# Two decode layers in one kernel: P times V of layer one in the wide form, its buffers in one arena slot, and the score mask as one matmul

## The chip, the cores and the metric

The kernel runs on one core of a Trainium2 chip. The metric is the device time of one execution in microseconds. It is compared as the median of several executions. The profile is one execution, seen by the hardware profiler; its span goes from the first to the last instruction of the program.

## What is computed

Two identical layers over a batch of four single tokens (`B = 4`, `Sq = 1`, `D = 512`), each an attention over a sliding window of a cached K and V and then a gated feed-forward block:

```python
W = min(4096, max(256, Sk // 4))          # 2048 of 8192 positions
rep = Hq // Hkv                           # 32 query heads, 8 kv heads: 4
q = (x @ wq) ...                          # 32 heads of 128
k = jnp.repeat(k_cache[:, :, Sk - W:, :], rep, axis=1)
v = jnp.repeat(v_cache[:, :, Sk - W:, :], rep, axis=1)
scores = einsum("bhqd,bhkd->bhqk", q, k) * (Dh ** -0.5)
p = softmax(scores, axis=-1)
o = einsum("bhqk,bhkd->bhqd", p, v) ... @ wo
...
x = x + A(layernorm(x));  x = x + B(layernorm(x))    # and both once more
# B: h = sigmoid(x @ w_gate) * (x @ w_up);  h @ w_down      (F = 1792)
```

The inputs are bfloat16. Both layers read the same cache and the same weights.

## The kernel before

**Data.** One head's K for all four tokens is two tiles of 1 MB (one a pair of tokens), the same for V. All of K (16 MB) is kept on the chip for both layers in its own 32 half tiles ("slots") of the `arena`. The other 18 slots make nine tiles, which `_SlotPool` gives out in turn to the query weights, V, the output projection `wo` (four tiles of two heads each, kept for both layers) and the feed-forward weights. Layer two runs the heads backwards and takes a few V tiles that layer one left in place; one V tile is put aside in PSUM during the feed-forward block ("stash": four transposes by DVE, line 568, and two half ones, line 585).

**The DMA queue.** All loads are issued by SP from line 398, in the order of one list (`loads`). `fill` takes loads from its head as long as a slot is free; a load whose slot is still read waits on SP for the last reader's semaphore, and everything behind it waits too. Around the end of layer one there are no free tiles, and some loads have a fixed place (`homes`): the two halves of the tiles named `Y`, `Z` (V of the last head), `GA` and `GB` (the two tiles of the first gate weights). The list of layer one goes: V of head 6, V of head 7 (two tiles each), gate weights (two tiles), up weights (four halves), down weights (four pieces), then the query weights of layer two.

**The order of the work.** The kernel emits operations in a program order; `_schedule` then simulates the engines with estimated durations and gives each engine its own order, which is fixed in the program. An operation with an earlier start goes first, one with an earlier place in the program wins a tie. Operations on one PSUM bank from different engines are ordered by `banks=`.

**Layer one** (`attn_first`). For each head h: DVE transposes K in place (`k_transpose`, line 830, four operations); the query is spread (line 818, ACT copies it, line 823); four mask matmuls (line 848) and sixteen score matmuls (line 859) of 32 columns with 512 moving columns fill one PSUM bank; DVE takes the maximum (lines 872 to 884), ACT the exponential (line 887); `turn_p` permutes P by a matmul (line 900), copies it (ACT, line 902) and transposes it (DVE, line 907). The sums go through four small GpSimd operations, three matmuls (line 926) and a reciprocal (line 933). The loop runs two heads ahead: `front(h + 2)`, then P times V of head h, then `turn` of head h + 2, then the output projection of head h.

P times V of layer one is **narrow** (`pv_unit`, line 949): for each pair of tokens 32 matmuls with a 128 x 128 block of V as the stationary operand and 8 columns of P moving; then a product with the reciprocals (DVE, line 957), four matmuls (line 967), a masked product (DVE, line 972) and 16 matmuls of the output projection (`wo_unit`, line 1137), which all heads add up in bank `WB`.

**Layer two** uses the **wide** form for seven of its eight heads (`pv_wide`, line 1033): 16 matmuls with 32 columns of P stationary and 512 columns of V moving, for both pairs at once; then a transpose of the bank (DVE, line 1041), a reduction (1046), a copy across partitions (1048), two GpSimd operations (`ad` 1050, `av` 1053), two small matmuls (`tr`, 1067), an ACT copy (1073) and four wide matmuls of the output projection (`wo_wide`, 1086). When the last of these is done, `wo_copy` (ACT, 1113) and `wo_back` (four fp32 matmuls, 1123) bring the result back to bank `WB`; the last heads use `wo_compact` (line 1102). The sums of the wide form (`sums`) need one GpSimd operation, one fp32 matmul (1008), a reciprocal (1010) and one more GpSimd operation (`rm`, 1013). Its buffers (`wide_buffers`) are doubled and lie in a tile of query weights that is no longer needed.

Of the kernel before, what the change touches and what calls it, by code (L numbers as in the profile page):

```python
# [278 lines left out]
def build(nc, A_x, A_k, A_v, A_wq, A_wo, B_wg, B_wu, B_wd, out, cfg=None):  # L279
# [16 lines left out]
    NJ = W // 128  # L296
# [25 lines left out]
    with es:  # L322
# [19 lines left out]
        msk_s = sb("msk_s", [128, 32], BF16)  # L342
        msk_m = sb("msk_m", [128, 2], BF16)
        psm = sb("psm", [128, 2], F32)
        rinv = sb("rinv", [128, 2 * NR], F32)
        onb = sb("onb", [128, 2 * NR], BF16)
        onp = sb("onp", [128, 2 * REP * NR], BF16)
# [73 lines left out]
        GB = ("wg", 1, 0)  # L421
# [122 lines left out]
        def load_glu(k):  # L544
            for nm, src in (("wg", wg_d), ("wu", wu_d)):
                if k == 0 and nm == "wu":
                    for c in range(NC):
                        load_half((nm, c, k), src[:, c, :], "bw_3k", F, ((Y, 0), (Y, 1), (Z, 0), (GA, 0))[c])
                    continue
                for cc in range(NC // 2):  # L550
                    load((nm, cc, k), 2, "bw_3k", (2 * F, src[:, 2 * cc:2 * cc + 2, :], False))
            on_free[GA] = lambda s: hfree.add(s + 1)
            on_free[GB] = lambda s: hfree.add(s + 1)
            for (a, b) in bounds_of(k):
                if k == 0:
                    load_half(("wd", a, k), wd_d[:, a:b, :].rearrange("p k n -> p (k n)"), "bw_4k", (b - a) * D,
                              ((GA, 1), (GB, 0), (GB, 1), (Y, 0))[a // 4])
                else:
                    load(("wd", a, k), 1, "bw_8k", ((b - a) * D, wd_d[:, a:b, :], False))
# [55 lines left out]
        P.op("vector", "zero_o", 1100.0, lambda v: v.memset(ps[:, OBS[0]:WB + 1, :], 0.0), w=[("o0",)], banks=OBS + (WB,))  # L615
# [3 lines left out]
        for jh in range(2):  # L619
            for bp in range(2):  # L620
                for i in range(2):
# [10 lines left out]
             lambda g: g.affine_select(msk_s[:, :].rearrange("p (i y) -> p i y", i=2),  # L632
                                       ones_f[:, :].rearrange("p (i y) -> p i y", i=2),
                                       [[1, 2], [0, NR]], ALU.is_equal, 0.0, base=-1, channel_multiplier=1),
# [202 lines left out]
        def softmax_unit(tag, hk, wait=False, q=True, between=None):  # L837
# [7 lines left out]
            def e_m(pe):  # L845
                last = None
                for gi in range(4):
                    last = pe.matmul(ps[32 * gi:32 * gi + 32, bank, :], msk_s[:, :],  # L848
                                     msk_m[:, :].unsqueeze(1).broadcast_to([128, 256, 2]), start=True, stop=False)
                return last  # L850

            def e_s(pe):
                last = None if wait else e_m(pe)
                for cp in range(4):
                    for gi in range(4):
                        jh, bp = gi // 2, gi % 2
                        kt = kpair(hk, bp).rearrange("p (j c k t) -> p c t j k", c=2, k=32, t=2)
                        q0 = ((k2 * 4 + cp) * 2 + bp) * 32
                        last = pe.matmul(ps[32 * gi:32 * gi + 32, bank, :], qbd[:, q0:q0 + 32],  # L859
                                         kt[:, cp // 2, cp % 2, jh * NJ:(jh + 1) * NJ, :], start=False, stop=(cp == 3))  # L860
                return last
# [36 lines left out]
        def turn_p(L, tag, k2, pb, wide=False):  # L898
# [10 lines left out]
            if L == 0:  # L909
                sums_old(tag, k2)  # L910

        def sums_old(tag, k2):
# [18 lines left out]
            rv = rinv[:, k2 * NR:(k2 + 1) * NR]  # L931
# [4 lines left out]
        def pv_unit(tag, h, k2, tiles, between=None):  # L936
            ob = OBS[k2]
            ev = ebuf[:, k2 * 256:(k2 + 1) * 256].bitcast(BF16).rearrange("p (m x t) -> p t m x", x=32, t=2)
            for n, (bp, name) in enumerate(tiles):
# [4 lines left out]
                def e_pv(pe, s=s, bp=bp):  # L944
                    last = None
                    src = tile_ap(s)
                    for j in range(2 * NJ):
# [7 lines left out]
            ov = onb[:, k2 * NR:(k2 + 1) * NR]  # L955
# [4 lines left out]
                     rinv[:, k2 * NR:(k2 + 1) * NR].rearrange("p (b r) -> p b r", r=REP), ALU.mult),  # L960
                 r=[("pso", k2, bp) for bp in range(2)] + [("rinv", k2)], w=[("on", k2)], banks=(ob,))
            op = onp[:, k2 * REP * NR:(k2 + 1) * REP * NR]
# [18 lines left out]
        def wide_buffers(s, op):  # L981
            f = tile_ap(s).bitcast(F32)
            n = 0
            for name, size in (("tv", 512), ("o32", 32), ("osh", 32), ("rm", 64), ("rv", 8), ("pr", 8)):
                for k2 in range(2):
# [4 lines left out]
            for k2 in range(2):  # L990
                rest["A", k2] = f[:, n:n + 128].bitcast(BF16)
                n += 128
            rest["op"] = op
            rest["mb"] = f[:, n:n + 64]
            P.op("gpsimd", "mb", 200.0,
                 lambda g: g.tensor_copy(rest["mb"].rearrange("p (b x) -> p b x", b=2),
                                         maskb.unsqueeze(2).broadcast_to([128, 2, 32])),
                 r=[("maskb",)], w=[("mb",)], after=(op,))

        def sums(tag, k2):  # L1000
            pr, rv, rm = (rest[n, k2] for n in ("pr", "rv", "rm"))
            P.op("gpsimd", "pr" + tag, 200.0,
                 lambda g: g.tensor_scalar(pr, sel_r[:, :], psm[:, k2:k2 + 1], None, ALU.mult),
                 r=[("psm", k2), ("sel_r",)], w=[("pr", k2)], after=(rest["op"],))
            sbank, c0 = (CB, 256) if tag in ("2.0", "2.%d" % (NW - 1)) else (WB, k2 * 8)
            out_ = ps[0:64, sbank, c0:c0 + 8]
            P.op("tensor", "sb" + tag, tm["pe_f32"],
                 lambda pe: pe.matmul(out_, rest["mb"], pr, start=True, stop=True),
                 r=[("pr", k2), ("mb",)], w=[("psb", k2)], banks=(sbank,))
            P.op("vector", "ri" + tag, c_dve(8) + 60.0, lambda v: v.reciprocal(rv[0:64, :], out_),  # L1010
                 r=[("psb", k2)], w=[("rinv", k2)], banks=(sbank,))
# [4 lines left out]
                 r=[("rinv", k2), ("maske",)], w=[("rm", k2)])  # L1016

        def pv_wide(tag, h, k2, tiles):
# [19 lines left out]
            for bp, name in tiles:  # L1038
                done(name)
            tv, o32, osh, rm, av = (rest[n, k2] for n in ("tv", "o32", "osh", "rm", "A"))  # L1040
            P.op("vector", "tv" + tag, c_dve(512), lambda v: v.transpose(tv, ps[:, ob, :]),  # L1041
                 r=[("pso", k2, 0), ("pso", k2, 1)], w=[("tv", k2)], banks=(ob,), after=(rest["op"],))

            def e_rd(v):
                dg = rest["dg", k2].rearrange("p (m y) -> p m y", m=4)[:, :, 0:128].rearrange("p m (q z) -> p q z m", z=32)[:, :, 0:8, :]
                return v.tensor_reduce(o32.rearrange("p (q x) -> p q x", x=8), dg, AXX, ALU.add)
            P.op("vector", "rd" + tag, c_dve(128), e_rd, r=[("tv", k2)], w=[("o32", k2)])
            P.op("vector", "sh" + tag, tm["dve_small"], lambda v: v.tensor_copy(osh[0:64, :], o32[64:128, :]),
                 r=[("o32", k2)], w=[("osh", k2)])
            P.op("gpsimd", "ad" + tag, 250.0, lambda v: v.tensor_tensor(o32[0:64, :], o32[0:64, :], osh[0:64, :], ALU.add),  # L1050
                 r=[("o32", k2), ("osh", k2)], w=[("o32", k2)])
# [5 lines left out]
                 r=[("o32", k2), ("rm", k2)], w=[("av", k2)])  # L1057
            late["tr", tag] = lambda: o_back(tag, k2, av)

        def o_back(tag, k2, av):  # L1060
            q0 = 16 + k2 * 16
            tb = CB if tag in ("2.%d" % (NW - 1), "2.%d" % (NW - 2)) else WB
# [7 lines left out]
            P.op("tensor", "tr" + tag, 2 * tm["pe_pair"], e_tr, r=[("av", k2), ("selm",)], w=[("pst", k2)], banks=(tb,))  # L1070
# [39 lines left out]
        def wo_copy():  # L1110
            k2 = (NW - 3) % 2
# [4 lines left out]
        def wo_back():  # L1116
            k2 = (NW - 3) % 2
            wr = rest["tv", k2]

            def e_b(pe):  # L1120
                last = None
                for c in range(NC):
                    last = pe.matmul(ps[:, WB, c * NR:c * NR + NB], wr[:, c * 128:(c + 1) * 128],
                                     selw[:, :], start=(c == 0), stop=False, skip_group_check=True)
# [21 lines left out]
        def attn_first():  # L1146
            def front(h):
                k_transpose(h)
                softmax_unit("0.%d" % h, h)
                turn = lambda: turn_p(0, "0.%d" % h, h % 2, PBS[h % 2])  # L1150
                return turn
# [3 lines left out]
            for h in range(HKV):  # L1155
                tag = "0.%d" % h
                turn = front(h + 2) if h + 2 < HKV else None
                if h == HKV - 1:
                    stash(stashed)
                    need(Z)  # L1160
                    stash_half(0, "st3")
                op = pv_unit(tag, h, h % 2, v_tiles[(0, h)])
                if turn is not None:
                    turn()
                wo_unit(tag, h, op, h % 2, False, h == HKV - 1)
# [102 lines left out]
        def glu(k, b0, b1, last=False):  # L1268
# [31 lines left out]
            for n, nm in enumerate(("wg", "wu")):  # L1300
                for c in range(NC):
                    piece = k == 0 and n == 1
# [12 lines left out]
                    if k == 0 and n == 0 and c % 2 == 0:  # L1315
# [106 lines left out]

        fill()
# [79 lines left out]
```

## Time and profile before

| | |
|---|---|
| device time, median of 3 executions | 181.05 us (180.65 to 181.91) |
| span of the profiled execution | 178.8 us |
| difference of the two | 2.25 us |
| bytes read from HBM | 70.78 MB |
| mean rate over the span | 396 GB/s |
| output of the kernel issued | 177.1 us into the span |

The device times are those of three executions; the page does not say which of them, if any, was profiled. In the slices of the page a digit is the busy share in tenths. The engines are PE (TensorE; its weight loads are a row of their own, PEld), DVE (VectorE), ACT (ScalarE), POOL (GpSimd) and SP (SyncE, which issues nearly all DMAs). The span has four parts: the query projection of layer one up to some 15 us; attention of layer one to 107 us; the feed-forward block to 118 us; layer two from there, whose attention ends at about 165 us.

### The profile page before, as it was taken

To read this page: it belongs to the slowest core of one execution; us is meant where nothing else is said; L and a number is where in the kernel's file an instruction comes from. 1 tells how busy PE (TensorE), PEld (TensorE's weight loads), DVE (VectorE), ACT (ScalarE), POOL (GpSimd) and SP (SyncE) were. 2 spreads that over 40 slices of the span, in tenths; PEclk is the share of its full clock that TensorE was granted. 3 is DMA by queue.
4 is the path that set the end of the run, shared out by engine and by line. 5 is a ranking of instruction groups with operands and counts; after the bars stand their busy time and mean duration, and the time that the engine had idled before them with its cause. 6 is when DMAs were issued, how large, how long until landed. Compare 5 with 4: busy or idle time off the path is not lost.

```text
span 178.8 us, 3879 instructions
## 1 busy us (share of the span) xinstructions
PE 101.7 (57%) x1641; PEld 55.1 (31%) x1653; DVE 104.4 (58%) x256; ACT 32.7 (18%) x87; POOL 21.5 (12%) x87
## 2 busy tenths in 40 slices
PE   0635326481933626506436857455886999766743
PEld 0202101241521412403414743231322444435311
DVE  7308997838476384593564483324199999751431
ACT  2002031221030300301102001000143455430101
POOL 6100010101010100100101000000011543351000
PEclk9999999999999999999999999999999999975555
DMA  5999999999999999999999999999999999999980
GB/s 184 418 429 427 422 423 416 414 422 420 422 413 419 420 423 422 411 421 422 423 411 420 414 401 387 407 360 421 410 395 418 423 420 422 412 418 402 410 353 22
DMA packets 12802, 71.05 MB, mean 397 GB/s; under 512 B 1256, under 2 KB 1264, under 8 KB 6640
## 3 DMA queue, kind: packets, MB, share of 16 engines
q1 hardware_dynamic: 12776, 70.79, 96.9%
q8 instruction: 13, 0.21, 0.5%
q14 instruction: 5, 0.04, 0.1%
q10 hardware_dynamic: 8, 0.00, 0.0%
HBM read 70.78 MB, written 0.00 MB: 396 GB/s over the span
## 4 chain that ended last, share of the span: by engine, by line
DMA 35%; DVE 33%; PE 19%; SPq 4%; issue 4%; ACT 2%; POOL 1%; DVEq 0%; ACTq 0%
DMA arena<-in_A_v_cache_dram 20%; DVE arena L830 11%; DMA arena<-in_B_w_down_dram 9%; PE ps L859 7%; DVE nmax L872 5%; DMA arena<-in_A_wq_dram 5%; SPq L398 4%; PE ps L949 3%; DMA arena<-in_B_w_up_dram 2%; PE ps L848 2%; DVE arena L1041 2%; DVE nmax L876 2%; DVE ebuf L907 2%; DVE mxt L880 2%; PE ps L1137 1%
## 5 line engine op out<-in xcount | busy, mean ns | idle before, releaser
L830 DVE STREAM_TRANSPOSE arena<-arena 128x1024 f32<-128x1024 f32 x32 | 37.0, 1202 | 0.0
L859 PE MATMUL ps<-arena,qbd 128*32 128x512 bf16 x256 | 25.8, 539 | 0.0
L949 PE MATMUL ps<-ebuf,arena 128*128 128x8 bf16 x576 | 17.8, 168 | 9.2 <-DMA arena<-in_A_v_cache_dram 6.1
L872 DVE TENSOR_REDUCE nmax<-ps 128x1 f32<-128x512 f32 x16 | 10.8, 676 | 19.9 <-PE ps L859 19.8
L848 PE MATMUL ps<-msk_m,msk_s 128*32 128x512 bf16 x64 | 8.6, 526 | 23.0 <-DVE arena L830 21.8
L949 PEld LDWEIGHTS ps<-ebuf,arena 128*128 128x128 bf16 x576 | 16.8, 104 | 11.3 <-DMA arena<-in_A_v_cache_dram 7.3
L887 ACT ACTIVATE prow<-ps,nmax 128x512 bf16<-128x512 f32 x16 | 11.0, 687 | 35.1 <-DVE nmax L884 29.5
L823 ACT CAST qbd<-ps 128x256 bf16<-128x256 f32 x16 | 5.9, 370 | 45.4 <-PE ps L859 35.2
L916 POOL CAST s<-psm 128x1 bf16<-128x1 f32 x9 | 1.7, 188 | 84.1 <-ACT prow L887 84.1
L859 PEld LDWEIGHTS ps<-arena,qbd 128*32 128x32 bf16 x256 | 8.4, 122 | 10.6 <-issue 7.8
L902 ACT CAST prow<-ps 128x512 bf16<-128x512 f32 x16 | 9.4, 586 | 9.9 <-PE ps L949 2.1
L769 PE MATMUL ps<-arena,xn 128*4 128x512 bf16 x64 | 8.3, 575 | 5.0 <-DMA arena<-in_A_wq_dram 4.7
L907 DVE STREAM_TRANSPOSE ebuf<-prow 128x256 f32<-128x256 f32 x16 | 7.0, 435 | 3.8 <-ACT prow L902 3.7
L848 PEld LDWEIGHTS ps<-msk_m,msk_s 128*32 128x32 bf16 x64 | 1.7, 98 | 24.0 <-DVE arena L830 22.6
L1309 PE MATMUL ps<-arena,xn 128*4 128x448 bf16 x64 | 7.2, 559 | 3.4 <-DMA arena<-in_B_w_up_dram 2.3
L818 PE MATMUL ps<-qh,eyew 32*128 32x64 bf16 x64 | 5.6, 217 | 4.8 <-ACT qbd L823 2.4
L746 ACT ACTIVATE lnv<-ps 128x4 f32<-128x4 f32 x4 | 0.7, 174 | 41.5 <-PE ps L742 41.5
L1033 PE MATMUL ps<-arena,ebuf 128*32 128x512 bf16 x112 | 7.4, 384 | 0.2 <-DVE nmax L884 0.2
L957 DVE TENSOR_TENSOR onb<-ps,rinv 128x16 bf16<-128x16 f32 x9 | 1.7, 185 | 9.7 <-PE ps L949 9.7
L784 DVE STREAM_TRANSPOSE ebuf<-ps 128x512 f32<-128x512 f32 x3 | 2.2, 717 | 8.4 <-PE ps L769 8.2
L1137 PE MATMUL ps<-onp,arena 128*128 128x16 bf16 x144 | 5.3, 175 | 2.4 <-DVE onp L972 2.4
L818 PEld LDWEIGHTS ps<-qh,eyew 32*128 32x128 bf16 x64 | 3.3, 106 | 9.8 <-ACT qbd L823 5.4
(111 smaller groups left out, 131.1 us busy)
## 6 DMA issues: line engine op xcount, KB each, us to landing
arena<-in_A_v_cache_dram SPq DMA_DIRECT2D x27, 1024.0 KB, 21.4
arena<-in_A_k_cache_dram SPq DMA_DIRECT2D x16, 1024.0 KB, 25.1
arena<-in_A_wq_dram SPq DMA_DIRECT2D x6, 1024.0 KB, 8.4
arena<-in_A_wo_dram SPq DMA_DIRECT2D x4, 1024.0 KB, 24.7
arena<-in_B_w_gate_dram SPq DMA_DIRECT2D x4, 896.0 KB, 16.3
arena<-in_B_w_down_dram SPq DMA_DIRECT2D x4, 512.0 KB, 6.4
arena<-in_A_wq_dram SPq DMA_DIRECT2D x4, 512.0 KB, 8.2
arena<-in_A_v_cache_dram SPq DMA_DIRECT2D x4, 512.0 KB, 6.8
```

Source lines behind the costliest of these rows:

```text
L769: last = pe.matmul(ps[32 * hh:32 * hh + NB, qb, :], xn[:, c * NB:(c + 1) * NB], src[:, o + hh * 512:o + (hh + 1) * 512], start=(c == 0), s ...
L818: last = pe.matmul(dst[:, :, a * REP:(a + 1) * REP], eyew[32 * hh:32 * hh + 32, 96 - 32 * a:224 - 32 * a], src, start=True, stop=True)
L830: P.op("vector", "T%d_%d" % (h, t), c_dve(1024), lambda v, v32=v32: v.transpose(v32, v32), r=[("slot", 4 * h + t)], w=[("slot", 4 * h + t)])
L848: last = pe.matmul(ps[32 * gi:32 * gi + 32, bank, :], msk_s[:, :], msk_m[:, :].unsqueeze(1).broadcast_to([128, 256, 2]), start=True, stop= ...
L859: last = pe.matmul(ps[32 * gi:32 * gi + 32, bank, :], qbd[:, q0:q0 + 32], kt[:, cp // 2, cp % 2, jh * NJ:(jh + 1) * NJ, :], start=False, s ...
L872: lambda v: v.tensor_reduce(nmax[:, k2:k2 + 1], ps[:, bank, :], AXX, ALU.max),
L887: lambda a: a.activation(prow[:, :].rearrange("p (m x t) -> p m x t", x=32, t=2), ps[:, bank, :].rearrange("p (m t x) -> p m x t", x=32, t ...
L902: P.op("scalar", "pc" + tag, c_act(512), lambda a: a.copy(prow[:, :], ps[:, pb, :]), r=[("ppb", pb)], w=[("prow",)], banks=(pb,))
L907: P.op("vector", "pt" + tag, c_dve(256), lambda v: v.transpose(et, prow[:, :].bitcast(F32)), r=[("prow",)], w=[("e", k2)])
L949: last = pe.matmul(ps[:, ob, bp * 8:bp * 8 + 8], src[:, j * 128:(j + 1) * 128], ev[:, j % 2, j % 16 // 2, x0:x0 + 8], start=(j == 0), stop ...
L1033: last = pe.matmul(ps[32 * g:32 * g + 32, ob, :], ew[:, g, mq, t], src.rearrange("p (m t d) -> p t m d", t=2, d=128)[:, t], start=(n == 0) ...
L1309: last = pe.matmul(ps[32 * g:32 * g + NB, gub[n], 0:NF], xn[:, c * NB:(c + 1) * NB], slot_ap(s)[:, g * NF:(g + 1) * NF], start=(c == 0), s ...
```

## The change

1. Heads 0 to 6 of layer one use `pv_wide`, `sums` and the wide tail; head 7 stays narrow. Heads 0 to 5 are projected by `wo_wide` into the PSUM bank `PBS[1]`, which `wo_copy(0)` and `wo_back(0, False)` then add to bank `WB`; head 6 uses `wo_compact`. Layer one's permuted P now always goes through bank `PBS[0]`; its sums and small transposes use bank `CB`, beside the spread query.
2. The buffers of the wide form take one half tile, and in layer one there is one set of them (`nbuf = 1`). The tile `GB` is taken from the pool at the very start; its first half holds the buffers, its second half is free for the third piece of the gate weights. The second gate tile of the first block becomes two half loads, the fourth piece in the first half of `GB`; it waits for the last reader of the buffers (`wide_done`). The down weights' places are reordered to fit. In layer two the two sets lie in the two halves of a tile. With one set, the row of reciprocals that `av` of head h reads (h up to 5) is the one that the sums of head h + 1 wrote last.
3. The score mask is one matmul with 128 stationary columns instead of four with 32, in both layers.

```diff
-        GB = ("wg", 1, 0)
+        GB = ("wide",)
...
                 for cc in range(NC // 2):
+                    if k == 0 and cc:
+                        for c in range(2, NC):
+                            load_half((nm, c, k), src[:, c, :], "bw_3k", F, (GB, NC - 1 - c))
+                        continue
                     load((nm, cc, k), 2, "bw_3k", (2 * F, src[:, 2 * cc:2 * cc + 2, :], False))
...
-                              ((GA, 1), (GB, 0), (GB, 1), (Y, 0))[a // 4])
+                              ((GA, 1), (GB, 1), (GB, 0), (Y, 0))[a // 4])
...
-                last = None
-                for gi in range(4):
-                    last = pe.matmul(ps[32 * gi:32 * gi + 32, bank, :], msk_s[:, :],
-                                     msk_m[:, :].unsqueeze(1).broadcast_to([128, 256, 2]), start=True, stop=False)
-                return last
+                return pe.matmul(ps[:, bank, :], msk_s[:, :],
+                                 msk_m[:, :].unsqueeze(1).broadcast_to([128, 256, 2]), start=True, stop=False,
+                                 skip_group_check=True)
...
             if L == 0:
-                sums_old(tag, k2)
+                (sums if wide else sums_old)(tag, k2)
...
+        def kb(tag, k2):
+            return 0 if tag[0] == "0" else k2
+
-        def wide_buffers(s, op):
-            f = tile_ap(s).bitcast(F32)
...
+        def wide_buffers(s, op, nbuf=2):
+            for k2 in range(nbuf):
+                f = slot_ap(s + k2).bitcast(F32)
...
-            sbank, c0 = (CB, 256) if tag in ("2.0", "2.%d" % (NW - 1)) else (WB, k2 * 8)
+            sbank, c0 = (CB, 256 + k2 * 8) if tag[0] == "0" or tag in ("2.0", "2.%d" % (NW - 1)) else (WB, k2 * 8)
...
-            tb = CB if tag in ("2.%d" % (NW - 1), "2.%d" % (NW - 2)) else WB
+            kk = kb(tag, k2)
+            q0 = (288 if tag[0] == "0" else 16) + k2 * 16
+            tb = CB if tag[0] == "0" or tag in ("2.%d" % (NW - 1), "2.%d" % (NW - 2)) else WB
...
         def attn_first():
+            s = base[GB]
+            begin = len(P.ops)
+            wide_buffers(s, P.ops[-1], 1)
+
             def front(h):
                 k_transpose(h)
                 softmax_unit("0.%d" % h, h)
-                turn = lambda: turn_p(0, "0.%d" % h, h % 2, PBS[h % 2])
-                return turn
+                return lambda: turn_p(0, "0.%d" % h, h % 2, PBS[0], h < HKV - 1)
+
+            def wide_done():
+                for o in P.ops[begin:]:
+                    if o.eng != "sync" and o.name[:2] in ("mb", "tv", "rd", "sh", "ad", "av", "tr", "pr", "sb", "ri", "rm", "wr"):
+                        P.readers.setdefault(("slot", s), []).append(o)
+                give(s)
...
                 if h == HKV - 1:
+                    wide_done()
                     stash(stashed)
                     need(Z)
                     stash_half(0, "st3")
-                op = pv_unit(tag, h, h % 2, v_tiles[(0, h)])
+                    op = pv_unit(tag, h, h % 2, v_tiles[(0, h)])
+                    wo_unit(tag, h, op, h % 2, False, True)
+                    continue
+                pv_wide(tag, h, h % 2, v_tiles[(0, h)])
                 if turn is not None:
                     turn()
-                wo_unit(tag, h, op, h % 2, False, h == HKV - 1)
+                op = late.pop(("tr", tag))()
+                if h < HKV - 2:
+                    wo_wide(tag, h, op, h % 2, h == 0, h == HKV - 3)
+                    if h == HKV - 3:
+                        wo_copy(0)
+                        wo_back(0, False)
+                else:
+                    wo_compact(tag, h, op, h % 2)
...
+        base[GB] = pool.alloc()
+        hfree.add(base[GB] + 1)
         fill()
```

The memset that clears PSUM banks at the start covers one bank more, and the mask's stationary operand is four times as wide; the small buffers of the narrow form (`rinv`, `onb`, `onp`) are no longer doubled.

## The prediction

> **What bounds the kernel now.** I read the page first, then the issues of the DMA queue in order of time, then the chain of waits, then single lines and narrow stretches.
>
> ```profile
> span 178.8 us, 3879 instructions
> ...
> PE 101.7 (57%) x1641; PEld 55.1 (31%) x1653; DVE 104.4 (58%) x256; ACT 32.7 (18%) x87; POOL 21.5 (12%) x87
> ...
> DMA  5999999999999999999999999999999999999980
> ...
> q1 hardware_dynamic: 12776, 70.79, 96.9%
> q8 instruction: 13, 0.21, 0.5%
> ```
>
> The DMA engines are busy from the second slice to the last but one; no compute engine passes 58%. 70.79 MB are moved and the change moves the same bytes. So the time is the stream's length plus some 3 us of tail, and an edit of compute counts only if it opens a hole in the stream, or closes one.
>
> Whether a hole can open is read from the issues on SP (start, length, what):
>
> ```profile
> 62.10 7.99 SPq L398 DMA_DIRECT2D arena<-in_A_v_cache_dram  x2
> 72.09 0.37 SPq L398 DMA_DIRECT2D arena<-in_A_wo_dram  x1
> 72.95 23.39 SPq L398 DMA_DIRECT2D arena<-in_A_v_cache_dram  x4
> 96.66 3.69 SPq L398 DMA_DIRECT2D arena<-in_B_w_gate_dram  x2
> 103.38 5.99 SPq L398 DMA_DIRECT2D arena<-in_B_w_up_dram  x4
> ```
>
> The four V loads from 72.95 (heads 6 and 7) wait for slots. The issues of single stretches (last column: us from issue to landing) at 83.45, 95.81 and 109.04 give how much was still queued:
>
> ```profile
> arena<-in_A_v_cache_dram SPq DMA_DIRECT2D x1, 1024.0 KB, 16.0
> arena<-in_A_v_cache_dram SPq DMA_DIRECT2D x1, 1024.0 KB, 8.6
> arena<-in_B_w_up_dram SPq DMA_DIRECT2D x1, 448.0 KB, 4.3
> ```
>
> So those landed at 99.45, 104.4 and 113.35, and the cover shrinks from 16 us to 4.3. A transfer makes no hole if it is issued early enough before the landing of the one ahead. The first transfer of all, issued at 0.79 into an idle queue, landed at 5.77; 1 MB takes 2.48 at the stream's pace, so 2.5 us of lead are enough. I call what exceeds 2.5 the margin.
>
> The chain of waits over that stretch (start, length, what):
>
> ```profile
> 92.51 0.62 PE ps L848 x4
> 93.12 1.71 PE ps L859 x14
> 94.83 0.96 PE ps L949 x32
> 95.81 8.63 DMA arena<-in_A_v_cache_dram
> 104.48 1.03 PE ps L949 x32
> ...
> 109.04 4.30 DMA arena<-in_B_w_up_dram
> ```
>
> Scores of head 7, PV of head 5, and at once the load of the last V, which takes the slot that this PV left: here slots are the link between compute and stream.
>
> **PE.**
>
> ```profile
> L859 PE MATMUL ps<-arena,qbd x256: 379/628/634, 21.2 to 151.8; 128*32 128x512 bf16 x128
> L1033 PE MATMUL ps<-arena,ebuf x112: 376/379/479, 135.6 to 158.8; 128*32 128x512 bf16 x112
> ```
>
> (min/median/max ns.) The same score matmul takes 628 ns before about 133 us and 379 after, although the page shows a granted clock of 9 tenths or more throughout layer one; the 16 of a head take 1.73–1.92 us there, 1.1 later. A wide PV is 16 matmuls of this shape: 1.05–1.15 in layer two (L1033), bounded above by 1.92 in layer one. I take 1.9, since it runs right behind such scores. The 64 narrow ones it replaces take 1.87 (94.76 to 96.63). PE gains nothing there. Mask: four column tiles take 0.62; one full-width matmul lies between 0.40 and 0.60 (L900, 128x512, late and early); gain 0 to 0.2 a head, on a PE that idles 4.4 us a head waiting for DVE's K transposes. Nothing: DVE covers it.
>
> The Trainium skill, "TensorE: Matmul & The Clock Gate", "Wait — 56ns, not 53.3ns?", gives 426.7 ns for back-to-back 512-column matmuls with the clock gate closed and 215.7 ns with it open. That agrees with 1.73/4 = 0.43 us per round of four column tiles in layer one, not with the page's clock row, and an estimate from it puts wide PV at 1.7 there against 0.86 in layer two; the sum would be the same.
>
> **Other engines, per wide head.** DVE gains the transpose (0.69), the reduce (0.43), the shift (0.18) and loses two products (0.20, 0.22): with the shorter reciprocal (0.18 for 0.24), +0.8 us, 5.7 over seven heads, into a DVE that idles about 4 us a head. POOL: four small ops of 0.19 become 0.31 + 0.30 + 0.25 + 0.67, about +0.8, with POOL nearly idle; but the sums need one POOL op before their matmul and not four, 0.6 us earlier. ACT: a copy of 0.18 a head, once 0.59. PE instructions: 7×(−48 PV −4 +2 −1) −72 (output projection) +8 −48 (mask) = −469 matmuls and as many weight loads.
>
> New wait on a shared bank: the query matmul of head h+3 now comes behind the whole wide tail of head h on bank CB. Tail after PV: 0.69+0.43+0.18+0.25+0.67+0.20+0.18 = 2.6, plus hand-overs 0.5, plus query and copy 0.8: 3.9 us. Head 4's PV would end near 84.4, scores 7 start at 92.5: hidden with 4 us to spare. Without that cover it would cost up to 3.9 a head.
>
> **Slots.** One of nine tiles is reserved from the start, so each V load waits for a release one tile later.
> - V loads of head 6: behind PV 4 (84.4) instead of 72.95; the queue lasts to 94.5. Hidden.
> - V loads of head 7: both behind PV 5. DVE's K transposes of head 7 began at 87.9, after a reciprocal that waited for POOL and PE. That can come up to 1 us earlier, or 0.9 later if the new DVE work lies in front; PV 5 ends at 95.7 to 97.6, I take 96.7, as now. The queue lasts to 99.45: lead 2.75, margin 0.25; at the late end 0.6 is lost.
> - First gate weights (now after V of head 6): behind PV 6. Its V lands at 99.45, so PV 6 ends 101.4; queue to 104.4: margin 0.5.
> - Gate piece 2 is free at once. Gate piece 3 waits for the last reader of the buffer slot, and on SP everything after it (up and down weights, wq) queues behind it. The single buffer also orders head 6's transpose behind the weight copy of heads 0–5: PV 5 (96.7) + tail 2.6 + projection 0.4 + copy 0.59 + four fp32 matmuls 0.95 + hand-overs 0.6 = 101.85. From there 0.69+0.43+0.18+0.25+0.67+0.20+0.5: 104.8. The queue then lasts to 104.4 + 2.23 + 1.11 = 107.8: lead 3.0, margin 0.5.
> - Up weights: the third waits for the second half stash (107.1 now), the fourth for the first gate matmuls (109.04; lead 3.2). DVE carries head 6's 1.3 us in this stretch; it had gaps of some 0.4 there, so +0.9: the fourth has 2.3 lead, 0.2 lost.
>
> **Instruction fetch.** Each of the 13 fetches on q8 is a 16 KB packet on one DMA engine. A transfer lands when its slowest engine is done: between the landings at 30.70 and 34.66, where the first fetch ran, 1 MB took 3.96 instead of 2.48. Later such bumps: 0.78 (landing at 121.2), 0.42 (133.0), 0.73 (137.5), 1.93 in all; two have a fetch beside them. 13 fetches for 3294 PE instructions are 253 each; 938 fewer are 3.7 fetches fewer, in layer one, where most change no landing. Bounds: 0 to −1.93; I take −0.3.
>
> The Trainium skill, "Runtime: NRT & Kernel Launch", "Instruction fetch mechanics", gives 256 instructions to a block and calls the crossing "mostly hidden". The 253 agree, the bump of 1.48 at the first fetch does not; by the rule this term would be 0 and the sum 181.3.
>
> **Sum.** 178.8 + 0.2 (fourth up weight) − 0.3 (fetch) = 178.7. The median of 181.05 is 2.25 above the span; the runs (180.65 to 181.91) don't say which is the profiled one. 178.7 + 2.25 = 180.95, say 181.0.
>
> **Rivals.**
> *The buffer slot holds back the stream.* If head 6's transpose lands on DVE behind the four stash transposes (101.97 to 104.47), its tail ends at 107.4, gate piece 3 is issued with 0.4 of lead and 2.1 us are lost; with the late PV 5 (0.6), the fourth up weight late (0.6) and one more late turn, up to 3.5. It decides from an issue of piece 3 later than 105.3. For: margins of 0.25 to 0.5 at three places, an order fixed by a planner's estimates. Against: the transpose comes earlier in program order. Alone: 181.05 + 2.1 = 183.15; to 184.6.
> *The late bumps go.* Fewer fetches leave the engines in step when the queue is shallow: −1.93, 179.1. For: the fetch at 134.9 hit an engine already behind. Against: layer two's own fetches stay.
> *It does not reach the stream at all:* 181.05, inside the forecast.
>
> **Chances.** 1% (1.8 us) is about what a measurement tells from no change. Forecast 0.60, own range 180.0 to 182.3; buffer slot 0.28, nearly all of it above 182.9; bumps 0.12, near 179.1. Faster 0.12, same 0.60, slower 0.28. For 8 in 10 I take 179.3 to 183.7: it leaves out about half of the fast case and, above, the third of the slow one with several late steps.
>
> **What would show it.** Right: PE near 1172 matmuls, 9 or 10 fetches, DVE near 110 us, the DMA row without a break; V of head 7 issued near 96.7; gate piece 3 before 105.3; last down weights landing near 175.7. Wrong: a slice below 9 between 95 and 120 us; score matmuls of layer one at 379 ns, which would shift all compute earlier; K transposes of head 7 far from 87.9; an order of DVE that I did not foresee.

## The result and the profile after

The changed kernel takes 190.41 us (median, 189.7 to 191.48) against 181.44 beside it on the same chip (180.65 to 182.16), six executions each. The ratio is 1.051, 95% interval 1.047 to 1.054: slower by 9.0 us, far above the range of 179.3 to 183.7. The profiled execution has a span of 188.6 us, 9.8 more than that of before (178.8, at the low end: in the later runs the kernel before had spans up to 180.4).

From the page of the changed kernel:

```profile
span 188.6 us, 3005 instructions
...
PE 109.6 (58%) x1184; PEld 45.8 (24%) x1184; DVE 110.8 (59%) x263; ACT 34.5 (18%) x95; POOL 27.1 (14%) x89
...
DMA  5999999999999999999880949999999999999990
GB/s 195 422 431 424 419 418 421 422 417 424 411 423 419 429 419 414 421 420 416 322 374 0 380 152 406 380 390 346 415 387 417 424 422 419 413 422 403 410 379 25
...
q1 hardware_dynamic: 12792, 70.79, 92.6%
q8 instruction: 9, 0.15, 0.3%
```

Work and bytes are about what was forecast: 1184 matmuls (1172 forecast), DVE 110.8 us, 9 instruction fetches, the same 70.79 MB. What is new is in the DMA row: two breaks, one of a whole slice with 0 GB/s. The last load landed at 175.69 before and at 185.51 now, 9.82 later. The whole loss lies in the stream.

The issues on SP around the breaks (start, length, what), to be held against those of before in the prediction:

```profile
68.88 8.27 SPq L398 DMA_DIRECT2D arena<-in_A_v_cache_dram  x2
77.19 0.60 SPq L398 DMA_DIRECT2D arena<-in_A_wo_dram  x1
91.65 11.82 SPq L398 DMA_DIRECT2D arena<-in_A_v_cache_dram  x4
110.60 3.12 SPq L398 DMA_DIRECT2D arena<-in_B_w_gate_dram  x3
113.76 5.28 SPq L398 DMA_DIRECT2D arena<-in_B_w_up_dram  x4
```

The four V loads are those of heads 6 and 7; inside the group the first of head 7 was issued at 102.29. All four follow the end of a wide PV: 91.60 (head 4) and 102.24 (head 5). Before, the last of them was issued at 95.81. The landings, put together from the issues and their times to landing:

| transfer | before: landed (after the one ahead) | after: issued | after: landed (after the one ahead) |
|---|---|---|---|
| V of head 6, second | 99.47 (2.49) | 92.23 | 99.23 (2.47) |
| V of head 7, first | 101.95 (2.48) | 102.29 | 107.54 (8.30) |
| V of head 7, second | 104.44 (2.49) | 102.87 | 111.39 (3.86) |
| gate, first | 106.67 (2.23) | 110.60 | 115.00 (3.60) |
| up, first | 110.02 (1.12) | 113.76 | 119.82 (2.56) |

The excess over before is 5.82 + 1.37 + 1.37 + 1.44 = 10.0 us, less 0.24 that the stream was ahead at the first row: 9.76 of the 9.82. It has three parts.

- The 5.82 is the first hole: the queue had been empty for 3.06 us when SP issued.
- The two 1.37 belong together, as a second hole of 2.74. SP issued the gate weights at 110.60, when fifteen of the sixteen DMA engines had been done with V since 109.93, and they landed 4.40 us later. In a run below that issued them with the queue just empty it was 4.43. The sixteenth engine was done with V only at 111.39, with an instruction fetch at 107.1 beside it. In step the gate weights take 2.23 us, so this engine alone would have finished them by about 113.6 (an estimate), before 115.00: the hole covered its lag.
- The 1.44 also has a fetch beside it (117.5). The last section comes back to the fetches.

Why did PV 4 end at 91.60, when its V had landed at 81.85? PE of the changed kernel (start, length, line; in brackets what ended the idle time before):

```profile
83.87 0.58 PE L849 MATMUL ps<-msk_m,msk_s 128*128 128x512 bf16 x1 [3.11 <-DVE arena L833]
84.39 1.90 PE L860 MATMUL ps<-arena,qbd 128*32 128x512 bf16 x16
88.85 0.61 PE L902 MATMUL ps<-prow,perm 128*128 128x512 bf16 x1 [2.57 <-ACT prow L889]
89.39 0.38 PE L1013 MATMUL ps<-arena 128*64 128x8 f32 x2
89.71 1.90 PE L1038 MATMUL ps<-arena,ebuf 128*32 128x512 bf16 x16
...
100.33 1.92 PE L1038 MATMUL ps<-arena,ebuf 128*32 128x512 bf16 x16
...
106.86 1.87 PE L1129 MATMUL ps<-msks,arena 128*128 128x4 f32 x8 [0.69 <-ACT arena L1120]
108.65 1.90 PE L1038 MATMUL ps<-arena,ebuf 128*32 128x512 bf16 x16
```

Behind the scores of head 6 PE has the permutation of P of head 6 (L902) first, which waits 2.57 us for the softmax; then the sums of head 6 (L1013); and only then PV 4 (L1038), which could have started at 86.28. PV 5 (100.33) comes right behind the scores of head 7, as before, and PV 6 (108.65, end 110.55) behind the four fp32 matmuls that bring the result of heads 0 to 5 back (L1129, eight rows); the first gate weights follow its end. DVE over the first turn:

```profile
87.71 0.21 DVE L886 TRANSPOSE_TENSOR_REDUCE nmax<-mxt 128x1 f32<-128x32 f32 x1
89.88 0.20 DVE L1015 RECIPROCAL arena<-ps 64x8 f32<-64x8 f32 x1 [1.96 <-PE ps L1013]
91.66 0.72 DVE L1047 STREAM_TRANSPOSE arena<-ps 128x512 f32<-128x512 f32 x1 [1.57 <-PE ps L1038]
...
93.03 0.45 DVE L909 STREAM_TRANSPOSE ebuf<-prow 128x256 f32<-128x256 f32 x1
93.40 4.58 DVE L833 STREAM_TRANSPOSE arena<-arena 128x1024 f32<-128x1024 f32 x4
```

The transpose of PV 4's result (L1047) stands in front of the K transposes of head 7 (L833). Those need nothing of PV 4 (K of head 7 had landed at 86.8), but each engine takes its queue in order. They started at 93.40, 5.5 us later than before (87.89), 3.7 of it from earlier heads and 1.8 from this turn. Before, the same place looked like this, first on PE and then on DVE:

```profile
80.55 1.93 PE L859 MATMUL ps<-arena,qbd 128*32 128x512 bf16 x16
82.41 1.01 PE L949 MATMUL ps<-ebuf,arena 128*128 128x8 bf16 x32
85.44 1.04 PE L949 MATMUL ps<-ebuf,arena 128*128 128x8 bf16 x32 [2.02 <-ACT prow L887]
...
86.52 0.19 DVE L957 TENSOR_TENSOR onb<-ps,rinv 128x16 bf16<-128x16 f32 x1 [2.41 <-PE ps L949]
```

DVE waited for PV 4 then as well, but for less: the first half of the narrow PV ran while the softmax was under way, so only 1.04 us of it came behind the gap, and DVE was idle 2.41 us there, not 3.5.

The starts of the score masks show where the time piles up. The turns from head 4 to 5 and from 6 to 7 take 14.25 us now and took 12.3 before: 3.8 of the 5.6 us by which head 7 is late. The other 1.8 had come by head 4, and no run here separates them.

| head | 2 | 3 | 4 | 5 | 6 | 7 |
|---|---|---|---|---|---|---|
| before | 35.65 | 46.11 | 56.49 | 68.79 | 80.15 | 92.51 |
| after | 36.36 | 47.09 | 58.43 | 72.69 | 83.87 | 98.12 |

Where the order comes from can be read in the estimates that the planner in the kernel's program works with (they are no measurements): they give both kernels the same end, 177.76 us. They count a wide PV as 0.99 us and a head's scores with their mask as 1.24. Layer one takes 1.90 and 2.4 (83.87 to 86.28). In the plan the scores of head 6 end at 76.89 and PV 4 can start at 80.55, when its V is there, so the permutation (79.07) goes first. On the chip V was there long before the scores were done, and the fixed order was the wrong way round.

### The profile page after: what moved, and what is told of

Its sections match the earlier page's. It is cut to its first block, busy times and chain, and to the rows that moved or that the text cites. A ratio compares the mean times of both kernels' runs of the same rounds, so it can differ in the third digit from the quotient of the medians.

```text
span 188.6 us, 3005 instructions
## 1 busy us (share of the span) xinstructions
PE 109.6 (58%) x1184; PEld 45.8 (24%) x1184; DVE 110.8 (59%) x263; ACT 34.5 (18%) x95; POOL 27.1 (14%) x89
## 3 DMA queue, kind: packets, MB, share of 16 engines
q1 hardware_dynamic: 12792, 70.79, 92.6%
## 4 chain that ended last, share of the span: by engine, by line
DVE 42%; PE 25%; DMA 21%; ACT 4%; issue 4%; POOL 1%; SPq 1%; DVEq 0%; ACTq 0%
DVE arena L833 17%; DMA arena<-in_A_wq_dram 10%; PE ps L860 9%; DMA arena<-in_B_w_down_dram 8%; PE ps L1038 6%; DVE nmax L874 4%; DVE arena L1047 4%; PE ps L849 3%; DMA arena<-in_B_w_up_dram 3%; DVE ebuf L909 2%; DVE arena L1053 2%; ACT prow L889 2%; DVE nmax L878 2%; DVE mxt L882 2%; PE ps L902 1%
## 5 line engine op out<-in xcount | busy, mean ns | idle before, releaser
L833 DVE STREAM_TRANSPOSE arena<-arena 128x1024 f32<-128x1024 f32 x32 | 36.8, 1201 | 0.0
L1038 PE MATMUL ps<-arena,ebuf 128*32 128x512 bf16 x224 | 21.2, 517 | 0.2 <-DVE nmax L886 0.2
L849 PE MATMUL ps<-msk_m,msk_s 128*128 128x512 bf16 x16 | 8.3, 517 | 20.0 <-DVE arena L833 18.6
L1047 DVE STREAM_TRANSPOSE arena<-ps 128x512 f32<-128x512 f32 x14 | 9.9, 704 | 10.8 <-PE ps L1038 10.4
L902 PE MATMUL ps<-prow,perm 128*128 128x512 bf16 x16 | 7.8, 485 | 14.5 <-ACT prow L889 14.4
L1008 POOL TENSOR_SCALAR arena<-sel_r,psm 128x8 f32<-128x8 f32 x14 | 4.3, 306 | 59.1 <-ACT prow L889 59.1
L1075 PE MATMUL ps<-msks,arena 64*128 64x8 bf16 x28 | 2.9, 171 | 13.2 <-POOL arena L1060 10.3
L860 PEld LDWEIGHTS ps<-arena,qbd 128*32 128x32 bf16 x256 | 6.7, 115 | 13.0 <-issue 11.1
L1060 POOL TENSOR_TENSOR arena<-arena 64x256 bf16<-64x256 f32 x14 | 9.3, 666 | 1.1
L1038 PEld LDWEIGHTS ps<-arena,ebuf 128*32 128x32 bf16 x224 | 6.8, 119 | 8.5 <-issue 6.9
L902 PEld LDWEIGHTS ps<-prow,perm 128*128 128x128 bf16 x16 | 1.6, 100 | 24.9 <-ACT prow L889 23.1
L1057 POOL TENSOR_TENSOR arena<-arena 64x32 f32<-64x32 f32 x14 | 3.5, 248 | 26.9 <-DVE arena L1055 26.7
```

Source lines behind the costliest of these rows:

```text
L833: P.op("vector", "T%d_%d" % (h, t), c_dve(1024), lambda v, v32=v32: v.transpose(v32, v32), r=[("slot", 4 * h + t)], w=[("slot", 4 * h + t)])
L849: return pe.matmul(ps[:, bank, :], msk_s[:, :], msk_m[:, :].unsqueeze(1).broadcast_to([128, 256, 2]), start=True, stop=False, skip_group_c ...
L902: lambda pe: pe.matmul(ps[:, pb, :], perm[:, :], prow[:, :], start=True, stop=True),
L1038: last = pe.matmul(ps[32 * g:32 * g + 32, ob, :], ew[:, g, mq, t], src.rearrange("p (m t d) -> p t m d", t=2, d=128)[:, t], start=(n == 0) ...
L1060: lambda v: v.tensor_tensor(av[0:64, :].rearrange("p (x q e) -> p x q e", x=8, q=4), o32[0:64, :].rearrange("p (q x) -> p x q", x=8).unsqu ...
```

## The experiments

The theory is that order on PE and DVE (**order**). The rivals: the tile that is missing from the pool (**slot**), and the one-matmul mask (**mask**). A run of the kernel before with nothing but the one-matmul mask gave no time: with the wider operand, 28 bytes were left for a buffer (`xn`) that needs 32.

**Permutation behind PV.** The changed kernel; the permutation of head h + 2 gets PV of head h as a predecessor.

```diff
-                 r=[("prow",)] + perms, w=[("ppb", pb)], banks=(pb,))
+                 r=[("prow",)] + perms, w=[("ppb", pb)], banks=(pb,), after=behind)
...
-                return lambda: turn_p(0, "0.%d" % h, h % 2, PBS[0], h < HKV - 1)
+                return lambda: turn_p(0, "0.%d" % h, h % 2, PBS[0], h < HKV - 1,
+                                      [o for o in P.ops if o.name == "PV0.%d" % (h - 2)])
```

> The changed kernel with one dependency more: in layer one the permutation matmul of head h+2 comes behind P times V of head h on PE. Theory ORDER (the loss comes from heads 2 and 4, whose wide PV stands behind the next softmax on PE, and with it the DVE transposes of the next K): the distance from the scores of head 4 to those of head 5, and from 6 to 7, falls from 14.3 us to 11 to 12, the scores of head 7 start near 93 instead of 98, V of head 7 is issued near 97 instead of 102.3, the empty slice near 100 us goes, 182 to 185 us. Theory SLOT (one tile fewer starves the queue whatever the order): 189 to 191, as the changed kernel.

Measured: 190.06, ratio 1.048 (1.043 to 1.053). That missed. The timeline of PE says why:

```profile
84.06 1.90 PE L860 MATMUL ps<-arena,qbd 128*32 128x512 bf16 x16
88.93 0.38 PE L1013 MATMUL ps<-arena 128*64 128x8 f32 x2 [2.97 <-POOL arena L1008]
89.24 1.90 PE L1038 MATMUL ps<-arena,ebuf 128*32 128x512 bf16 x16
```

The permutation is gone from in front of PV 4, but the sums matmul (L1013) now stands there, and it waits for the same softmax by way of POOL: idle 2.97 instead of 2.57. This run neither confirms nor refutes the order; it left one blocker in place.

**Permutation and sums behind PV.** The same, with `after=behind` on the sums matmul too.

```diff
-                 r=[("pr", kk), ("mb", kk)], w=[("psb", k2)], banks=(sbank,))
+                 r=[("pr", kk), ("mb", kk)], w=[("psb", k2)], banks=(sbank,), after=behind)
```

> The changed kernel; in layer one both the permutation and the sums matmul of head h+2 come behind P times V of head h on PE (the first attempt moved the permutation alone, and the sums matmul, which waits for the same softmax, stood in front of PV instead). Planner durations as in the change. Theory ORDER: scores 4 to 5 and 6 to 7 are 11 to 12.5 us apart, V of head 7 issued before 98, 182 to 185 us. If something else holds the even heads back (the DVE transposes behind the wide tail, whatever PE does): 14 us apart still and 188 to 191.

Measured: 184.56 (184.28 to 185.61), ratio 1.021 (1.017 to 1.024). It is 3.3 us above the kernel before beside it, so two ordering edges take away 5.7 of the 9.0 us. The masks start at 80.61 (head 6) and 91.81 (head 7), V of head 7 is issued at 95.88, and it lands 2.49 after the one ahead: the first hole is gone. The second is there: first gate weights issued at 104.30, just as V landed (104.32), and landed 4.41 after it instead of 2.23.

**The planner with measured durations.** The changed kernel; only two estimates differ.

```diff
-            P.op("tensor", "S" + tag, (16 if wait else 20) * tm["pe_row"], e_s,
+            P.op("tensor", "S" + tag, 2300.0 if tag[0] == "0" else (16 if wait else 20) * tm["pe_row"], e_s,
...
-            P.op("tensor", "PV" + tag, 16 * tm["pe_row"], e_pv,
+            P.op("tensor", "PV" + tag, 1900.0 if tag[0] == "0" else 16 * tm["pe_row"], e_pv,
```

> The changed kernel; only the durations that the planner assumes for layer one's scores and wide PV are the measured ones (2.3 and 1.9 us instead of 1.24 and 0.99), which alters the fixed order of the engines and nothing else. Theory ORDER: the planner itself then puts PV before the permutation for heads 2 and 4; 182 to 185 us. Theory SLOT: 189 to 191.

Measured: 183.19 (182.08 to 183.44), ratio 1.008 (1.005 to 1.012). Its PE and DVE at the same place:

```profile
78.78 1.90 PE L860 MATMUL ps<-arena,qbd 128*32 128x512 bf16 x16
81.86 1.90 PE L1038 MATMUL ps<-arena,ebuf 128*32 128x512 bf16 x16 [1.18 <-DMA arena<-in_A_v_cache_dram]
...
85.64 4.55 DVE L833 STREAM_TRANSPOSE arena<-arena 128x1024 f32<-128x1024 f32 x4
```

PV 4 now waits for its V and nothing else, and the K transposes of head 7 begin at 85.64, 2.3 us earlier than in the kernel before. 7.2 of 9.0 us came of two numbers in the planner.

**The slot alone.** The kernel before, with the tile reserved from the start and the gate and down weights placed as in the change; all heads narrow.

```diff
-        GB = ("wg", 1, 0)
+        GB = ("wide",)
...
+        base[GB] = pool.alloc()
+        hfree.update((base[GB], base[GB] + 1))
```

> The kernel before (narrow PV, four mask matmuls), with only the tile taken from the pool at the start and the gate pieces and down weights placed as in the change; nothing lies in the tile. Theory SLOT: the V loads of head 7 come late, 186 to 190 us. Theory ORDER: the two halves of a narrow PV still free their tiles around the softmax, V of head 7 is issued by 97, 180.5 to 182.5 us.

Measured: 181.71, ratio 1.002 (0.999 to 1.005). One tile less costs nothing that shows as long as the masks keep their times (head 7 at 92.22): V of head 7 is issued at 95.52 and 96.38 and lands in step. So the missing tile is not the cause by itself. It takes lead away (both loads of head 7 wait for PV 5), so that a late PV 5 opens a hole. Whether the same lateness would be free with the ninth tile was not tried. An estimate from the rows above says no: the first load of head 7 would then follow PV 4 (91.60) and land in step at 101.7, but the second would still be issued at 102.29 and land some 5.25 later, as the first did here. That leaves a hole of about 3.3 us instead of 5.8.

**The old mask.** The kernel with the measured durations, and four mask matmuls of 32 columns again.

```diff
-                return pe.matmul(ps[:, bank, :], msk_s[:, :],
-                                 msk_m[:, :].unsqueeze(1).broadcast_to([128, 256, 2]), start=True, stop=False,
-                                 skip_group_check=True)
+                for gi in range(4):
+                    last = pe.matmul(ps[32 * gi:32 * gi + 32, bank, :], msk_s[:, :],
+                                     msk_m[:, :].unsqueeze(1).broadcast_to([128, 256, 2]), start=True, stop=False)
```

> The kernel with the planner's measured durations (183.2 us) with the mask as four 32-column matmuls again. All theories: within 0.5 us of 183.2. If the mask as one matmul cost or gained on PE, more than 1 us away.

Measured: 182.89, ratio 1.011 (1.007 to 1.016), against 1.008 with the one matmul. The two intervals overlap (they reach 0.6 to 0.8 us to either side), so no effect of the mask shows. The two runs were on different chips.

**The corrected planner on the kernel before.** Only the estimate for the scores is altered, by the first of the two edits above.

> The kernel before; only the planner's duration for layer one's scores is the measured 2.3 us. It tells whether a corrected plan speeds up any kernel or only mends the order that the wide form got. Theory ORDER: the stream of the kernel before has no hole, so 180.5 to 182 us. Rival (a better plan is worth some us by itself): below 179.5.

Measured: 180.99, ratio 1.000 (0.997 to 1.003). The estimate was just as wrong before and did no harm; it became a fault only with the wide PV.

**The second hole.** In the version with the measured durations PE reads, from the scores of head 7 on:

```profile
92.54 1.87 PE L1038 MATMUL ps<-arena,ebuf 128*32 128x512 bf16 x16
...
99.06 1.87 PE L1129 MATMUL ps<-msks,arena 128*128 128x4 f32 x8 [0.69 <-ACT arena L1120]
100.85 1.90 PE L1038 MATMUL ps<-arena,ebuf 128*32 128x512 bf16 x16
```

The four fp32 matmuls that bring back heads 0 to 5 (eight rows of L1129) stand in front of PV 6, after whose end (102.75) the first gate weights are issued. V of head 6 had landed at 99.25. The edit sends all wide heads through the compact projection, so that copy and fp32 matmuls fall away:

```diff
-                if h < HKV - 2:
-                    wo_wide(tag, h, op, h % 2, h == 0, h == HKV - 3)
...
-                else:
-                    wo_compact(tag, h, op, h % 2)
+                wo_compact(tag, h, op, h % 2)
```

> The kernel with the planner's measured durations (183.2 us), and heads 0 to 5 of layer one projected by the 16 compact matmuls instead of four wide ones, so that the ACT copy and the four fp32 matmuls that bring the wide result back are gone. Theory: the rest of the loss (1.7 us) is PV of head 6 waiting on PE behind those fp32 matmuls (99.1 to 100.9), so that the first gate weights are issued at 102.8 with 1.4 us of lead; without them PV 6 runs at 99.3, the issue is near 101.3, 180.8 to 182.3 us. Rival: the rest is the single buffer slot that holds back the last gate piece, or the wide tail on DVE in front of the stash: 183 or more.

Measured: 181.51 (180.86 to 183.49), ratio 1.004 (1.000 to 1.008). That was another chip than for the version with the measured durations, so both were run once more on one chip, and with them the old planner with the compact projection.

> The changed kernel with the measured durations of layer one in the planner, once more, so that it stands on the same chip beside the version with the compact projection. 183.2 as before; V of head 7 issued near 94.5, first gate weights near 102.8, behind the four fp32 matmuls.

> The same with the compact projection for all wide heads of layer one, on the same chip. Theory (the fp32 matmuls in front of the wide PV of head 6 open the second hole): 1.2 to 2.0 us less than the version beside it, so 181.2 to 182.0; first gate weights issued near 101.4. Rival (the difference of 1.7 us between the two earlier batches was one of chips): within 0.5 us of the version beside it.

> The changed kernel with its own planner estimates, and only the projection altered: all wide heads of layer one go through the compact form, so the ACT copy and the four fp32 matmuls that stood in front of the wide PV of head 6 are gone. Theory of two separate holes: scores, PV 4 and PV 5 keep their late places, so the loads of V of head 7 are issued near 102.3 us and the first hole (5.8 us) stays; the second (1.4 us, first gate weights) closes, since PV 6 can end near 108.1 at the latest. Span 188.6 - 1.4 = 187.2, time near 189.0. Rival (the fp32 matmuls also hold back the earlier heads): the first hole shrinks too and the time falls below 186. Rival (they cost nothing; the 1.4 us came of something else): 190.4, no change.

Measured: measured durations 183.23 (182.16 to 183.69), ratio 1.010 (1.007 to 1.014); with the compact projection 182.62 (181.55 to 183.51), ratio 1.007 (1.004 to 1.011); compact projection on the old plan 187.84 (187.21 to 188.91), ratio 1.037 (1.032 to 1.042). The DMA rows of the first two, in that order:

```profile
DMA  5999999999999999999999699999999999999980
```

```profile
DMA  5999999999999999999999899999999999999970
```

In these rows the slice of 6 becomes one of 8. With the compact projection the gate weights are issued at 101.56 instead of 103.00 and land in step (2.23): the hole closes, as expected. Its worth is not settled: 0.6 us on the same chip, between what was expected and what the rival allowed, and 1.5 to 1.7 across chips. In the two profiled executions on the same chip (183.03 both) the gain was lost again: at the first up weights the stream lies 2.25 us behind the kernel before without the compact projection and 0.69 with it, but the last loads land at 178.19 and 178.18. The executions of this version on the second chip lie at 181.55 to 181.79 and at 182.57 to 183.51, with nothing in between. The profiled one took 2.90 us instead of 1.27 for a transfer that landed at 123.25, with a fetch at 121.2 beside it, and 3.36 instead of 2.49 for one that landed at 159.82, with a fetch at 156.0; the one profiled on the first chip (181.43) took 1.87 there, and had its gate weights 3.22 behind V although they were issued at 101.44, with a fetch at 105.1.

On the old plan the compact projection gained 2.3 us against the kernel before beside each, or 2.6 by the two medians, where 1.4 was expected. V of head 7 was issued at 101.91 and the first hole stayed (7.73 between landings), so the rival that the fp32 matmuls hold back the earlier heads falls. The gate weights were issued at 107.35, 2.27 ahead of the landing before theirs, so there was hardly a hole left. The number expected was too small because it counted the second hole as the third row of the table alone (1.37), and not as the 2.74 of two rows. Not all of the 2.74 was gained: the gate weights still came 3.49 behind V instead of 2.23, with a fetch at 108.9 beside them and one engine 1.10 behind the other fifteen (113.11 against 112.01). Without a hole over it, the lag of one fetch showed. The first up weights, beside no fetch in this kernel, took 1.10 instead of 2.56.

No version is faster than the kernel before. In each of them the same 70.8 MB pass through the same queue, and in the kernel before no hole was left to close.

## Why the prediction was wrong

**What bounds the kernel: right.** The stream does; all of the loss is in four landings.

**PE, mask, other engines: right.** Wide PV takes 1.90 in layer one, as taken, and PE gains nothing; mask 0; DVE 110.8.

**Slots: the step that failed.** "Behind PV 4 (84.4) ... Hidden" was harmless: PV 4 ended at 91.60 and V of head 6 still landed on time. The next step was not: "DVE's K transposes of head 7 began at 87.9 ... That can come up to 1 us earlier, or 0.9 later if the new DVE work lies in front; PV 5 ends at 95.7 to 97.6, I take 96.7". The K transposes came 5.5 us later and PV 5 ended at 102.24, so a margin of 0.25 became the hole of 5.8. The error was to price the new DVE work in front at its own duration, 0.9 us, and not at what it waits for. It was the transpose of PV 4's result, and DVE stood idle for it from 87.92 to 91.66 but for one reciprocal of 0.20. That, in turn, depended on the order on PE, which was assumed: PV 4 right behind the scores of head 6, at 84.4. The page of before could have raised doubt: the narrow PV 4 ran in two halves around the softmax gap (82.41 and 85.44), with the permutation between them; one undivided PV has to go before or after it. Priced from the rows of before, "after" meant at least the 2 us of that gap for each head affected, and all that stands behind it on DVE.

**Gate weights behind PV 6, margin 0.5: mechanism seen, place wrong.** The text put the four fp32 matmuls in front of the transpose of head 6; they stood in front of PV 6 itself, and took 1.87 us and not the 0.95 of layer two. This opened the second hole, 2.74 us in the changed kernel and 0.94 in the version with the measured durations (3.17 instead of 2.23 between landings); with the compact projection it is gone.

**Instruction fetch, -0.3: wrong sign.** Nine fetches, as forecast at 9 or 10, yet the one at 117.5, just after the second hole, stands beside 1.44 us of loss. The one at 107.1, just after the first, made one engine 1.46 late, and the second hole covered that. By the cause inferred in the last section, what counts is where a fetch falls, not how many there are.

**The rivals.** The slower one, the buffer slot, had the right link (a slot released late, then a hole), but named gate piece 3, which was issued at 113.37 and landed in step. The slot without the wide PV costs nothing that shows. The faster rival, that the late bumps go, did not come either: from the first up weights to the last load the stream fell back by no more than in the kernel before (9.80 us behind at the one, 9.81 at the other), so their sum was the same 1.93. What decided was named only among the signs, "an order of DVE that I did not foresee", without a price; it should have been the rival.

## What to carry to other kernels

Where each engine has a fixed order, an operation that is put into a queue costs what it waits for, to everything behind it, not its own duration; look for the independent work that stands behind it. An order made from estimates is only as good as the durations it was made from, and joining several small operations into one takes away the places between them that hid a wrong estimate. When a change moves operations, compare the order on each engine, at the buffers that release transfers, before adding up durations.

## What the runs showed of the hardware

**A hole re-aligns the DMA engines, and the next instruction fetch then costs again.** A transfer lands when its slowest engine is done. In the changed kernel the sixteen engines finished the last output weights of layer one (94.28) over a stretch of 1.87 us. The V of head 6 behind them, issued with little more than that one transfer left in the queue, let the engines that were ahead run dry; they finished it over 0.43, and the slowest was on time (96.76). The first V of head 7, behind the hole, took 0.54, and the next, with the fetch at 107.1, 1.94: one engine alone was 1.46 behind the others. After the second hole the same: 0.43, then 1.87 with the fetch at 117.5. The fetch at 67.4, when the engines were spread already, made one landing 0.23 late, and the next took 0.14 less: so a hole gives the lag back, and the next fetch takes it anew. The other versions agree: in the two with measured durations and in the one with two ordering edges the spread behind the second hole was 0.53, 0.55 and 0.33, and the next fetch stands beside a landing 1.72, 1.42 and 1.79 us late. In the kernel before, the engines were 1.9 to 2.0 us apart when the fetches at 86.1, 99.0 and 105.6 came, and the landings beside them were in step to 0.03. The Trainium skill, "Runtime: NRT & Kernel Launch", section "Instruction fetch mechanics", calls the crossing of a block "mostly hidden"; here, in a kernel bound by its stream, two landings were 1.37 and 1.44 us late with a crossing beside them, though the second hole covered the first of these. The cause is inferred from the coincidence of fetch and lag in each trace; no run moved a fetch by itself.

**Ahead of its first record the clock row says nothing of the matmul rate.** The clock row of the changed kernel's page, and two windows of the changed kernel (start and end, length, busy time and count of each engine, then granted clock, DMA share, GB/s of each window):

```profile
PEclk9999999999999999955555555555559999985555
...
48.00:62.00 14.00, 7.68 (x62) 2.33 (x54) 8.87 (x18) 1.91 (x5) 1.50 (x4) 1.00 1.02 420
98.00:112.00 14.00, 10.43 (x99) 4.80 (x99) 4.61 (x14) 2.13 (x5) 1.61 (x6) 0.50 0.44 169
```

The clock reads 1.00 in the first and 0.50 in the second, and the chain of waits has the wide PV at about the same pace in both:

```profile
49.50 1.74 PE ps L1038 x16
...
108.72 1.86 PE ps L1038 x16
...
164.33 0.89 PE ps L1038 x16
```

In layer two it takes half of that. The trace of the changed kernel holds no clock record before 76.19 us, that of the kernel before none before 131.69, and the row counts time without a record as full clock. From 76.19 on, row and durations agree: the records give full clock to 79.60, half to 141.04 and full again to 168.35, and in the first of these stretches the permutation took 0.39 us instead of 0.61:

```profile
63.41 0.61 PE L902 MATMUL ps<-prow,perm 128*128 128x512 bf16 x1 [2.57 <-ACT prow L889]
...
77.67 0.39 PE L902 MATMUL ps<-prow,perm 128*128 128x512 bf16 x1 [1.10 <-ACT prow L889]
```

So ahead of the first record the durations are to be trusted, not the row, and the planner's estimates for scores and wide PV held for layer two only.
